# Second layer's quads reordered, its second block pair split in place, and the first layer's last outputs moved among them

## The chip, the cores and the metric

One core of one Trainium2 chip. The time is device microseconds (us) of one execution of the whole program; a kernel's time is the median of its runs.

## The reference

Retention (attention scores times a causal decay table, no softmax), then two feed-forward layers over 2304 tokens, model width 512, inner width 2048:

```python
scores = scale * np.matmul(q, k.transpose(0, 1, 3, 2))
ret = scores * Dmat[None, :, :, :]
x = np.matmul(ret, v)                      # to [2304, 512]
h = x @ w_in                               # layer 1
g = P(h) / (Q(h) + 1e-06)                  # cubic over 1 + |b0 h| + |b1| h^2
x = g @ w_out
h = x @ moe2_w_in                          # layer 2
g = s * (np.maximum(h, 0.0) ** 2) + b
return g @ moe2_w_out
```

## The kernel before, in words

Every fp32 operand of TensorE (PE) is held as two rounded parts, high and low, and a product is three matmuls: high by low, low by high, high by high (`three`, L377). To split a tile, ScalarE (ACT) copies it to the rounded type and VectorE (DVE) or GpSimd (POOL) subtracts (`lo_on`, L521). Weights come from DRAM as 64-bit words (`raw`); `w_round` (L132) turns them into fp32 in one ACT and three DVE instructions, `w_split` (L147) makes the two parts (ACT copy, POOL subtraction). A raw buffer is loaded again (`next_load`, on the SP queue) when its last reader, a POOL instruction, is done.

**Layer 1** runs 80 units (a token block of 512 or 256 by a slice of 128 inner columns). Unit u computes `h` (`emit_in`, 12 matmuls), then `rational` (L418, ACT, POOL, DVE) makes the parts of g, ending in `gl` on POOL (L436), and `out1` (L454) adds 12 matmuls to the outputs. The outputs of the last units have nothing else beside them: the program lists them first and the second layer behind.

**Layer 2** takes the weights in 16 quads (two slices of 128 by two token blocks of 512), `quad` (L702). Quads 0 to 7 are the first pass, tokens 0 to 1023; quads 8 to 15 the second, tokens 1024 to 2047. The last 256 tokens ride in the first pass (`tail_in`). Quads 0 and 8 are computed plainly (`hs`, 4 blocks of 12 matmuls); the others by seven products of 6 matmuls (`product`, Strassen-Winograd) over sums of blocks of x ("1" to "4") and of weights (S1 to S4). Product 1 goes to bank hA, is copied to hB by ACT, and product 2 adds to hA, so product 2 must wait for that copy. 5 and 6 use hG and hB; 3, 7, 4 add to them. Between products `fill(n)` puts n output groups (`out2`, 6 matmuls each) of the quad before; there are 10 per quad in the first pass and 8 in the second. TensorE's order here is pinned as written. ACT, DVE, POOL and the queues run in the order that a scheduler chose at build time, each strictly in order; `behind(...)` keeps an instruction behind another in that order.

In a first-pass quad the next quad's weights are rounded and split (`cut_first` after product 1, `cut_second` after product 6), the weight sums are built on POOL (`s_sums`, L589) and split (`s_split`, L600), and all are written to DRAM for the second pass (`w_keep`, `s_spill`). Quads 1 to 6 also prepare the second pass's x: `x_keep` (L554) splits a block through temporaries, half a block at a time, and spills it by four POOL-queue DMAs; `x_fetch` reads it back in quads 7 and 8. Sums of x blocks are accumulating DMAs of the POOL queue (`x_sum`, L536).

Of the kernel before, what the change touches and what calls it, by code (L numbers as in the profile page):

```python
# [42 lines left out]
def retention_ffn_kernel(ctx, tc, a, b, s2, b2, w, qkv, maskv, gdec, out):  # L43
# [3 lines left out]
    P = 128  # L47
# [99 lines left out]
    def w_split(kf, pinned=False):  # L147
        rest = tc.keep_in_program_order if pinned else free
        f = w_words(kf)[1].bitcast(F32)
        w_views(kf)  # L150
        i, j = w_place(kf)
        if kf < NF:
            t, n = w_halves[i]
            todo = [(f.rearrange("p (w x) -> p w x", w=2), t[:, :, n:n + 2, :])]
        else:
            todo = [(f[:, DM * x:DM * (x + 1)], w_half(y)) for x, y in enumerate((i, j))]
        for src, dst in todo:
            rest(nc.scalar.copy(dst[:, 0], src))  # L158
            nc.gpsimd.tensor_tensor(out=dst[:, 1], in0=src, in1=f32(dst[:, 0]), op=ALU.subtract)  # L159
# [163 lines left out]
    def ffn(fctx):  # L323
# [117 lines left out]

        def evac1(t0, m, f, e, ps):
# [99 lines left out]
        def x_split(pair, key):  # L542
            for c in range(2):
                h, l = (x[:, c, :] for x in both(key))
# [5 lines left out]
        KEYS = ("11", "12", "1", "22", "21", "3")  # L550
        NEXT = {"12": ("1",), "22": ("3", "2"), "21": ("4",)}
        x_spill = {}

        def x_keep(i, c):  # L554
            key = KEYS[i]
            if c == 0:
                x_spill[key] = spill.tile([P, 2, 2, 512], F32, name=f"xs{key}")
            at = x_at(1, key)[:, c, :]
# [5 lines left out]
            if c == 1:  # L564
                if key in ("11", "22"):
                    x_negate(1, key)
                for x in NEXT.get(key, ()):
                    x_sum(1, x)

        fetched = []  # L570

        def x_fetch(key):
            for x, y in enumerate(both(key, 1)):
                fetched[:] = [nc.gpsimd.dma_start(out=y, in_=x_spill[key][:, x])]
# [14 lines left out]
        def s_sums(q):  # L589
            w1, w2 = (w_words(NF + 2 * q + i)[1].bitcast(F32)[:, 0:DM] for i in range(2))  # L590
            a = {"11": w1[:, 0:256], "12": w1[:, 256:512], "21": w2[:, 0:256], "22": w2[:, 256:512]}
            t = [tmp_tile(2 * q + i, "tt") for i in range(2)]
            s1, s2, s3, s4 = t[0][:, 0:256], t[0][:, 256:512], t[1][:, 0:256], t[1][:, 256:512]
            nc.gpsimd.tensor_tensor(out=s1, in0=a["21"], in1=a["22"], op=ALU.add)
            nc.gpsimd.tensor_tensor(out=s3, in0=a["21"], in1=a["11"], op=ALU.subtract)
            nc.gpsimd.tensor_tensor(out=s2, in0=a["11"], in1=s1, op=ALU.subtract)
            nc.gpsimd.tensor_tensor(out=s4, in0=a["12"], in1=s2, op=ALU.add)
            return t
# [46 lines left out]
        def relu2(u, h, n, on_act):  # L645

            ta = tmp.pop(u, None)
            tt = h
            if ta is None:
                ta = tmp_tile(u, "ta", n)  # L650
            if h is ta or n < 512:
                tt = ta
            nc.scalar.activation(ta, h, AF.Relu)  # L653
            nc.scalar.activation(ta, ta, AF.Square)
            if on_act:
                nc.scalar.activation(tt, ta, AF.Identity, bias=b2_sb, scale=s2_sb)
            else:
                nc.vector.tensor_scalar(tt, ta, s2_sb, b2_sb, op0=ALU.mult, op1=ALU.add)
            gh, gl = g_tiles(u, n)
            return nc.scalar.copy(gh, tt), lo_on(nc.vector, gl, tt, gh)  # L660
# [41 lines left out]
        def quad(q, fills):  # L702
# [17 lines left out]
            if NQ // 2 - 1 <= q < NQ - 1:  # L720
                w_fetch(k + 2)
                w_fetch(k + 3)
            if NQ // 2 <= q < NQ - 1:
                with behind(*fetched):
                    s_fetch(q + 1)

            def prep(c):

                if q <= len(KEYS):
                    x_keep(q - 1, c)  # L730
# [9 lines left out]
            def cut_second():  # L740
# [3 lines left out]
                if rounds:  # L744
                    next(rounds[1], None)
                    w_split(k + 3)
                    t = s_sums(q + 1)
                    for x in (k + 2, k + 3):
                        del w_raw[x]
                        next_load()  # L750
                    with behind(*loads):
                        w_keep(k + 2)
                        w_keep(k + 3)
                    s_split(q + 1, t, 0)
                    return lambda: s_split(q + 1, t, 1)
                return lambda: None

            if q % (NQ // 2) == 0:
                while late:
                    late.pop(0)()  # L760
                fill(4)

                for (i, j), tag, key in zip(((0, 0), (0, 1), (1, 1), (1, 0)), ("hA", "hG", "hB", "hT"), ("1", "3", "2", None)):
# [6 lines left out]
                    done = relu2(("q", q, i, j), ps, 512, True)  # L770
                    with behind(*ends):
                        if key and first:
                            x_split(0, key)
                        if (i, j) == (0, 0):
                            cut_first()
                        if (i, j) == (0, 1):
                            cut_second()()
                    ends[:] = done
                    fill(4 if first else 2)
                    if first and (i, j) == (1, 1):  # L780
                        tail_in(q, 0, "o")
                with behind(*ends):
                    x_split(pas, "4")
                if not first:
                    x_fetch("1")
                    x_fetch("3")
# [5 lines left out]
            hB = ps_h.tile([P, 512], F32, tag=("hT", "hB")[q % 2], name=f"hB{q}")  # L792
# [3 lines left out]
            def renew(*keys):  # L796
                if last:
                    for x in keys:
                        x_fetch(x)
# [6 lines left out]
            product(q, 5, hG, True)  # L806
            g5 = tmp_tile(q, "tq")
            ends[:] = [nc.scalar.copy(g5, hG)]
            while late:
                late.pop(0)()  # L810
            fill(2)
            product(q, 6, hB, False)
            ends.append(nc.vector.tensor_tensor(out=hG, in0=hB, in1=g5, op=ALU.add))
            with behind(*ends):
                if last:
                    x_split(1, "2")
                cut_rest = cut_second()
            fill(2)
            product(q, 2, hA, False)
            ends[:] = relu2(("q", q, 0, 0), hA, 512, True)  # L820
            renew("21")
            with behind(*ends):
                prep(0)
            fill(1 + first)
            product(q, 3, hG, False)
            relu2(("q", q, 0, 1), hG, 512, True)
            renew("22")
            fill(1 + first)
# [3 lines left out]
            sum22 = nc.vector.tensor_tensor(out=tmp[u], in0=hB, in1=g5, op=ALU.add)  # L832
            relu2(u, tmp[u], 512, first)
            cut_rest()
            with behind(*ends):
                prep(1)
            fill(2)
# [4 lines left out]
            renew("12")  # L842
            ends[:] = [sum22, sum22]
# [4 lines left out]
        def outs_of(q):  # L848
            return [lambda j=j, e=e: out2(q, j, e) for j in (1, 0) for e in range(4)] + \
# [6 lines left out]
        for u in range(NU):  # L856
# [6 lines left out]
            for x in outs_at[u]:  # L863
                for e in range(NC):
                    out1(x, e)
            if final[0:1024].all() and sums:
# [12 lines left out]
        assert first_rounds and not sums  # L879
        rest = [lambda x=x, e=e: out1(x, e, pe) for x in outs_at[NU] for e in range(NC)]  # L880
# [93 lines left out]
```

## Time and profile before

| what | value |
|---|---|
| time, median of 3 runs | 878.95 us (877.92 to 880.23) |
| the profiled execution's own time | 880.4 us, span 878.6 us |
| granted TensorE clock, mean | 0.995 |
| busy: PE, DVE, ACT, POOL | 848.9, 612.2, 608.6, 439.5 us |

The span runs from the first instruction to the last. PE counts as busy while a matmul is in flight. A row of the trace gives start and duration in us, engine, line, operation, what it writes and reads, and in brackets how long the engine sat idle before it and what it waited for.

### The profile page before, as it was taken

The page shows a single profiled execution, that of the slowest core. Times are in us where ns is not written, and L with a number is a line of the kernel's source. Part 1 is how long each engine was busy: PE and PEld are TensorE (multiplying, and loading weights), DVE is VectorE, ACT ScalarE, POOL GpSimd, SP SyncE. Part 2 cuts the span into 40 slices and gives each one's busy share as a digit, 9 for nine tenths or more (in the row PEclk, how much of TensorE's full clock was granted, in tenths as well). Part 3 has the DMA queues.
Part 4 walks back from the last instruction along what each step waited for, and adds up shares of the span by engine and source line. Part 5 has one row for each costly group of instructions (what it writes and reads, how often), then busy time and mean ns, then how long its engine had stood idle before and what let it go on. Part 6 is the DMA issues. An engine that isn't in the chain of part 4 may idle for free.

```text
span 878.6 us, 12889 instructions
## 1 busy us (share of the span) xinstructions
PE 848.9 (97%) x4812; PEld 715.1 (81%) x4812; DVE 612.2 (70%) x892; ACT 608.6 (69%) x1027; POOL 439.5 (50%) x381
## 2 busy tenths in 40 slices
PE   6989999999999999999998999999989999999998
PEld 5988788788888888888886787878778888888886
DVE  3886886997888887968958856777777423444445
ACT  1333998986878876778878788786767657444553
POOL 2795564575665664656767734555357511111100
PEclk9999999999999999999999999999999999999999
DMA  9992110111111100101113268655889994444402
GB/s 342 371 351 117 49 49 1 48 48 49 49 41 57 49 19 30 48 1 49 48 48 60 42 234 305 216 185 201 290 286 370 401 348 150 144 144 144 144 1 96
DMA packets 44207, 123.59 MB, mean 141 GB/s; under 512 B 4464, under 2 KB 4976, under 8 KB 39152
## 3 DMA queue, kind: packets, MB, share of 16 engines
q1 hardware_dynamic: 28096, 81.86, 25.8%
q0 software_dynamic: 16048, 40.90, 15.3%
q8 instruction: 38, 0.62, 0.3%
q14 instruction: 25, 0.20, 0.1%
HBM read 83.42 MB, written 35.13 MB: 135 GB/s over the span
## 4 chain that ended last, share of the span: by engine, by line
PE 70%; DVE 10%; DMA 6%; ACT 6%; POOL 4%; issue 3%; SPq 0%; POOLq 0%; ACTq 0%; DVEq 0%
PE o L380 19%; PE h L380 18%; PE p L380 15%; PE hB L380 4%; DMA raw<-in_w_dram 3%; PE hG L380 3%; PE hA L380 3%; DVE wm L141 2%; PE sc L239 2%; PE pv L270 2%; DVE raw L144 2%; POOL w L159 2%; PE pv L262 1%; PE hs L380 1%; ACT wm L138 1%
## 5 line engine op out<-in xcount | busy, mean ns | idle before, releaser
L380 PE MATMUL h<-xh,w 128*128 128x512 f32 (+1 forms) x640 | 184.7, 370 | 0.0
L380 PE MATMUL o<-gh,w 128*128 128x512 f32 (+1 forms) x592 | 166.4, 367 | 0.0
L424 POOL TENSOR_TENSOR tq<-tq,ta 128x512 f32<-128x512 f32 (+1 forms) x80 | 100.5, 1256 | 99.6 <-ACT tq L423 99.3
L380 PEld LDWEIGHTS h<-xh,w 128*128 128x128 f32 x640 | 117.4, 190 | 20.6
L380 PE MATMUL p<-w,gh 128*128 128x512 f32 x336 | 122.8, 391 | 0.0
L683 DVE TENSOR_TENSOR acc<-acc,p 128x512 f32<-128x512 f32 x126 | 85.2, 683 | 53.6 <-PE p L380 52.1
L380 PE MATMUL h<-xl,w 128*128 128x512 f32 (+1 forms) x320 | 119.2, 372 | 3.3 <-DVE tt L433 3.2
L380 PEld LDWEIGHTS o<-gh,w 128*128 128x128 f32 x592 | 106.9, 189 | 18.0
L159 POOL TENSOR_TENSOR w<-raw,w 128x512 fp32r<-128x512 f32 (+1 forms) x48 | 84.4, 1764 | 55.7 <-ACT w L158 47.9
L436 POOL TENSOR_TENSOR gl<-tt,gh 128x512 fp32r<-128x512 f32 (+1 forms) x74 | 93.3, 1262 | 35.4 <-ACT gh L435 24.8
L380 PE MATMUL o<-gl,w 128*128 128x512 f32 (+1 forms) x296 | 108.3, 367 | 1.5 <-POOL gl L436 1.5
L380 PE MATMUL p<-w,gx 128*128 128x512 f32 x360 | 99.0, 391 | 0.2 <-ACT ta L653 0.2
L380 PEld LDWEIGHTS p<-w,gx 128*128 128x128 f32 x360 | 67.9, 189 | 14.8 <-ACT ta L653 0.7
L431 DVE SCALAR_TENSOR_TENSOR tt<-tt,aneg,h 128x512 f32<-128x512 f32 (+1 forms) x80 | 55.1, 689 | 35.5 <-ACT h L430 34.9
L380 PEld LDWEIGHTS p<-w,gh 128*128 128x128 f32 x336 | 63.4, 189 | 13.2
L380 PEld LDWEIGHTS h<-xl,w 128*128 128x128 f32 x320 | 60.6, 189 | 15.3 <-DVE tt L433 2.9
L426 DVE TENSOR_TENSOR tt<-tt,h 128x512 f32<-128x512 f32 (+1 forms) x80 | 50.2, 628 | 27.6 <-ACT tt L425 27.4
L428 ACT ACTIVATE ta<-tq,lnb 128x512 f32<-128x512 f32 (+1 forms) x80 | 54.6, 682 | 18.3 <-POOL tq L424 18.0
L380 PE MATMUL p<-w,gl 128*128 128x512 f32 x168 | 65.8, 391 | 1.0 <-DVE gl L522 1.0
L380 PEld LDWEIGHTS o<-gl,w 128*128 128x128 f32 x296 | 55.8, 189 | 11.0 <-POOL gl L436 1.9
L423 ACT ACTIVATE tq<-ta,babs 128x512 f32<-128x512 f32 (+1 forms) x80 | 61.9, 774 | 3.8 <-DVE h L432 3.8
L619 POOL DMA_DIRECT2D w<-ws x32 | 22.8, 712 | 82.9 <-PE hA L380 30.5
(137 smaller groups left out, 1815.6 us busy)
## 6 DMA issues: line engine op xcount, KB each, us to landing
raw<-in_w_dram SPq DMA_DIRECT2D x32, 1024.0 KB, 5.6
ws<-w SPq DMA_DIRECT2D x32, 512.0 KB, 11.1
w<-ws POOLq DMA_DIRECT2D x32, 512.0 KB, 5.7
xT<-in_qkv_dram SPq DMA_DIRECT2D x16, 576.0 KB, 8.4
sf<-ss POOLq DMA_DIRECT2D x7, 1024.0 KB, 5.2
xs<-tt POOLq DMA_DIRECT2D x24, 256.0 KB, 6.7
vn<-in_qkv_dram SPq DMA_DIRECT2D x16, 320.0 KB, 8.5
out_dram<-acc SPq DMA_DIRECT2D x18, 256.0 KB, 3.5
```

The source lines that it names most:

```text
L141: rest(nc.vector.scalar_tensor_tensor(out=t, in0=t, scalar=3, in1=lo, op0=ALU.logical_shift_left, op1=ALU.bitwise_or))
L144: rest(nc.vector.scalar_tensor_tensor(out=hi, in0=hi, scalar=0x80000000, in1=t, op0=ALU.bitwise_and, op1=ALU.bitwise_or))
L159: nc.gpsimd.tensor_tensor(out=dst[:, 1], in0=src, in1=f32(dst[:, 0]), op=ALU.subtract)
L380: yield nc.tensor.matmul(ps, lhsT=lh, rhs=rh, start=start and x == 0, stop=stop and x == 2, skip_group_check=True)
L423: nc.scalar.activation(tq, ta, AF.Identity, bias=babs[:, 0:1], scale=babs[:, 1:2])
L424: nc.gpsimd.tensor_tensor(out=tq, in0=tq, in1=ta, op=ALU.mult)
L426: nc.vector.tensor_tensor(out=tt, in0=tt, in1=h, op=ALU.mult)
L428: nc.scalar.activation(ta, tq, AF.Ln, bias=lnb, scale=QS)
L431: nc.vector.scalar_tensor_tensor(out=tt, in0=tt, scalar=aneg[:, 0:1], in1=r, op0=ALU.add, op1=ALU.mult)
L436: nc.gpsimd.tensor_tensor(out=gl, in0=tt, in1=f32(gh), op=ALU.subtract)]
L619: nc.gpsimd.dma_start(out=w_half(i), in_=w_spill[kf - NF, x])
L683: nc.vector.tensor_tensor(out=at, in0=at, in1=ps, op=ALU.add)
```

## The change

Five parts. (1) In the Strassen quads product 2 comes right after product 1 and two fills; the order is 1, 2, 5, 6, 3, 7, 4, with fills 2, 2, 2, 2, 1 in the first pass and 2, 1, 1, 2, 2 in the second. (2) `cut_first` moves behind product 6 and `cut_second` behind product 7; within it the first half of the weight sums is split before the second weight tile. (3) `x_keep`, `x_fetch` and their spill are gone: quad 7 splits "11", "21", "22", "12" of the second pair straight into the slots that its own products have left, issues the block sums there, and quad 8 splits "1", "3", "2", "4"; quad 8's blocks run in another order, with its outputs between. (4) The outputs of the last three units of layer 1 become fills of quad 0 (`hs00` runs ahead of most of them); some of the last splits go from POOL to DVE (`tail_lo`), and the third and fourth block sums are issued later. (5) A layer-1 weight tile is subtracted on POOL in two halves.

```diff
         if kf < NF:
             t, n = w_halves[i]
-            todo = [(f.rearrange("p (w x) -> p w x", w=2), t[:, :, n:n + 2, :])]
+            nc.scalar.copy(t[:, 0, n:n + 2, :], f.rearrange("p (w x) -> p w x", w=2))
+            for x in range(2):
+                dst = t[:, :, n + x, :]
+                nc.gpsimd.tensor_tensor(out=dst[:, 1], in0=f[:, DM * x:DM * (x + 1)], in1=f32(dst[:, 0]), op=ALU.subtract)
+            return
...
-                nc.gpsimd.tensor_tensor(out=xl[:, e, r], in0=at, in1=f32(xh[:, e, r]), op=ALU.subtract)
+                tail_lo[:] = [lo_on(nc.vector if m < 512 or e % 2 else nc.gpsimd, xl[:, e, r], at, xh[:, e, r])]
...
-        def x_keep(i, c):
-            key = KEYS[i]
...
-            h, l = (tmp_tile(4 * i + 2 * c + x, "tt").bitcast(F32R) for x in range(2))
-            nc.scalar.copy(h, at)
-            lo_on(nc.gpsimd, l, at, h)
-            for x, y in enumerate((h, l)):
-                nc.gpsimd.dma_start(out=x_spill[key][:, x, c], in_=f32(y))
...
+                    t = s_sums(q + 1)
+                    s_split(q + 1, t, 0)
                     w_split(k + 3)
-                    t = s_sums(q + 1)
                     for x in (k + 2, k + 3):
                         del w_raw[x]
                         next_load()
...
+                tags = ("hA", "hB", "hG", "hT") if first else ("hA", "hT", "hG", "hB")
+                order = ((0, 0), (0, 1), (1, 1), (1, 0)) if first else ((0, 0), (1, 0), (0, 1), (1, 1))
...
+                    if not first:
+                        split = relu2(("q", q, i, j), ps, 512, True, wait=True)
+                        fill((4, 4, 2, 0)[n])
+                        done = split()
...
             product(q, 1, hA, True)
-            ends[0] = nc.scalar.copy(hB, hA)
-            with behind(*ends):
-                cut_first()
-            renew("11")
+            nc.scalar.copy(hB, hA)
+            while late:
+                late.pop(0)()
+            n1, n2, n3, n4, n5 = (2, 2, 2, 2, 1) if first else (2, 1, 1, 2, 2)
+            fill(n1)
+            product(q, 2, hA, False)
+            split = relu2(("q", q, 0, 0), hA, 512, True, wait=True)
+            fill(n2)
+            ends[:] = split()
+            if last:
+                with behind(*ends):
+                    x_split(1, "11")
+                    x_negate(1, "11")
+                x_sum(1, "1")
+                with behind(*ends):
+                    x_split(1, "21")
             product(q, 5, hG, True)
...
+            fill(n3)
             product(q, 6, hB, False)
...
+            with behind(*ends):
+                cut_first()
+            fill(n4)
             product(q, 3, hG, False)
...
             product(q, 7, hB, False)
...
+            with behind(*ends):
+                cut_second()
             relu2(u, tmp[u], 512, first)
...
+            fill(n5)
             if first:
                 tail_in(q, 0, "o")
             product(q, 4, hB, False)
...
-            if final[0:1024].all() and sums:
+            if final[0:1024].all() and len(sums) > (1 if u == NU - 1 else 2):
...
-        rest = [lambda x=x, e=e: out1(x, e, pe) for x in outs_at[NU] for e in range(NC)]
+        rest = [lambda x=x, e=e: out1(x, e, pe) for x in range(NU - 3, NU) for e in range(NC)]
```

Three places in the order. **TensorE, end of layer 1** (o74 and o77 are output banks of units 74 to 78, hs00 and hs01 blocks of quad 0, gl78/gh78 and gx parts of g). Before:

```order
L380 MATMUL o77_2_4763<-gx_4106,w4_1052 128x512 x3
L380 MATMUL o77_3_4764<-gx_4106,w4_1052 128x512 x3
L380 MATMUL o77_0_4761<-gl78_4710,w0_80 128x512
L380 MATMUL o77_0_4761<-gh78_4709,w0_80 128x512 x2
L380 MATMUL o77_1_4762<-gl78_4710,w0_80 128x512
```

Now:

```order
L383 MATMUL hs00_4792<-xh_78,w0_80 128x512 x2
L383 MATMUL o74_0_4638<-gx_4122,w0_80 128x512 x3
L383 MATMUL o74_1_4639<-gx_4122,w0_80 128x512 x3
L383 MATMUL o74_2_4640<-gx_4122,w0_80 128x512 x3
L383 MATMUL o74_3_4641<-gx_4122,w0_80 128x512 x3
L383 MATMUL o77_0_4822<-gx_4122,w4_1055 128x512 x3
L383 MATMUL o77_1_4823<-gx_4122,w4_1055 128x512 x3
L383 MATMUL o77_2_4824<-gx_4122,w4_1055 128x512 x3
L383 MATMUL o77_3_4825<-gx_4122,w4_1055 128x512 x3
L383 MATMUL hs01_4838<-xl_79,w0_80 128x512
```

A block of quad 0 now stands before the outputs of unit 76, another between those of units 77 and 78.

**ACT, turn from quad 2 to quad 3** (ta, tt temporaries, ht the tail's bank, raw23 and w0 the weight tile of quad 3). Before:

```order
L653 ACTIVATE ta115_5545<-hB2_5262 128x512
L660 CAST gh114_5495<-ta114_5491 128x256
L654 ACTIVATE ta115_5545<-ta115_5545 128x512
L653 ACTIVATE ta117_5553<-ht5_5505 128x256
L656 ACTIVATE hB2_5262<-ta115_5545,b2_sb_75,s2_sb_74 128x512
L802 COPY hB3_5519<-hA3_5518 128x512
```

Now:

```order
L640 CAST gx_4122<-ta116_5407 128x512
L634 ACTIVATE ta114_5471<-ta114_5471,b2_sb_75,s2_sb_74 128x256
L161 CAST w0_80<-raw23_5184 128x512 x2
L640 CAST gh114_5475<-ta114_5471 128x256
L631 ACTIVATE ta115_5516<-hB2_5264 128x512
L785 COPY hB3_5507<-hA3_5506 128x512
```

The copy of hA to hB comes one instruction after the read of the last quad's hB, not five, and the casts of the second weight tile now stand ahead of it.

**SP queue, a first-pass quad** (ss3 the spilled weight sums of quad 3, ws40 to ws43 spilled weight parts, raw24 and raw25 loads for quad 4). Before:

```order
L608 DMA ss3_5352<-xh_78 128x512
L126 DMA raw25_5340<-in_w_dram 128x1024
L608 DMA ss3_5352<-xl_79 128x512
L126 DMA raw24_5085<-in_w_dram 128x1024
L614 DMA ws40_5087<-w0_80 256x1x512
```

Now:

```order
L586 DMA ss3_5420<-xh_78 128x512
L126 DMA raw25_5429<-in_w_dram 128x1024
L126 DMA raw24_5186<-in_w_dram 128x1024
L592 DMA ws40_5188<-w0_80 256x1x512
L592 DMA ws41_5190<-w4_1055 256x1x512
```

The two loads now follow each other directly.

## Rows read from the trace of the kernel before

**Rows 1.** The page: busy us of each engine over the span (share), instructions.

```profile
PE 848.9 (97%) x4812; PEld 715.1 (81%) x4812; DVE 612.2 (70%) x892; ACT 608.6 (69%) x1027; POOL 439.5 (50%) x381
```

**Rows 2.** Busy time by stretch: start:end, length, engines, PE clock, DMA share, GB/s.

```profile
82.03:470.66 388.63, 385.29 (x1861) 324.75 (x1861) 315.26 (x483) 322.18 (x532) 240.48 (x181) 1.00 0.11 39
470.66:500.85 30.19, 26.73 (x134) 22.18 (x133) 25.52 (x37) 21.63 (x41) 20.88 (x20) 1.00 0.37 70
500.85:696.37 195.52, 187.61 (x885) 154.93 (x884) 135.57 (x173) 149.83 (x267) 103.14 (x112) 0.99 0.79 267
696.37:863.67 167.30, 167.30 (x740) 138.56 (x739) 75.22 (x115) 90.37 (x148) 21.79 (x32) 1.00 0.49 157
863.67:878.60 14.93, 11.04 (x49) 8.82 (x47) 6.24 (x10) 2.60 (x4) 0.00 (x0) 0.94 0.38 142
```

**Rows 3.** Waits of PE: who for whom, us in total, times, longest.

```profile
PE hB L380 <- DVE ta L832: 2.8, 3, 1.1
PE hG L380 <- DVE xl L522: 2.7, 2, 2.5
...
PE o L380 <- POOL gx L436: 2.0, 1, 2.0
...
PE o L380 <- POOL gl L436: 1.5, 1, 1.5
```

**Rows 4.** PE in order of time: first matmul of quads 6, 7 and 8.

```profile
639.92 0.40 PE L380 MATMUL hA<-xl,w 128*128 128x512 f32 x1
...
670.33 0.40 PE L380 MATMUL hA<-xl,w 128*128 128x512 f32 x1
...
696.37 0.63 PE L380 MATMUL p<-w,gx 128*128 128x512 f32 x2
```

**Rows 5.** ACT: a raw tile's landing starts the rounding, two quads in turn.

```profile
569.04 1.16 ACT L138 ACTIVATE wm<-raw 128x1024 f32<-128x1024 f32 x1 [2.85 <-DMA raw<-in_w_dram]
...
596.60 1.17 ACT L138 ACTIVATE wm<-raw 128x1024 f32<-128x1024 f32 x1 [3.00 <-DMA raw<-in_w_dram]
```

**Rows 6.** POOL, quad 3: from the weight sums' start to their last; one spilled split between.

```profile
580.07 0.86 POOL L594 TENSOR_TENSOR tt<-raw 128x256 f32<-128x256 f32 x1 [3.50 <-DVE raw L144]
...
584.96 1.74 POOL L522 TENSOR_TENSOR tt<-acc,tt 128x512 fp32r<-128x512 f32 x1
586.64 0.56 POOL L563 DMA_DIRECT2D xs<-tt  x1
587.22 0.75 POOL L597 TENSOR_TENSOR tt<-raw,tt 128x256 f32<-128x256 f32 x1
```

**Rows 7.** SP queue, the same place: issues of the two raw loads.

```profile
585.02 0.33 SPq L126 DMA_DIRECT2D raw<-in_w_dram  x1
...
588.00 0.33 SPq L126 DMA_DIRECT2D raw<-in_w_dram  x1
```

**Rows 8.** DVE: one operation alone, and beside a busy POOL.

```profile
570.24 1.22 DVE L141 SCALAR_TENSOR_TENSOR wm<-wm,raw 128x1024 uint32<-128x1024 uint32 x1
...
575.52 2.14 DVE L141 SCALAR_TENSOR_TENSOR wm<-wm,raw 128x1024 uint32<-128x1024 uint32 x1 [1.13 <-ACT wm L138]
...
639.93 2.88 DVE L522 TENSOR_TENSOR gx<-ta,gx 128x512 fp32r<-128x512 f32 x1 [1.80 <-ACT gx L660]
```

**Rows 9.** PE and ACT, quad 3: end of product 1, and the copy that product 2 needs.

```profile
558.72 0.39 PE L380 MATMUL hG<-xl,xh 128*128 128x512 f32 x1
...
562.36 0.55 ACT L802 COPY hB<-hA 128x512 f32<-128x512 f32 x1
```

**Rows 10.** ACT groups, 500 to 697 us: count, busy, mean ns.

```profile
L158 ACT CAST w<-raw 128x512 fp32r<-128x512 f32 x26 | 16.0, 664 | 12.7 <-DVE raw L144 12.7
...
L681 ACT COPY acc<-p 128x512 f32<-128x512 f32 x10 | 6.0, 616 | 0.0
```

**Rows 11.** POOL groups, layer 1: a weight tile's subtraction, whole and half.

```profile
L159 POOL TENSOR_TENSOR w<-raw,w 128x1024 fp32r<-128x1024 f32 x13 | 32.9, 2532 | 6.6 <-ACT w L158 6.5
...
L159 POOL TENSOR_TENSOR w<-raw,w 128x512 fp32r<-128x512 f32 x4 | 5.3, 1317 | 1.2 <-ACT w L158 1.2
```

More of the change, by code (lines that the diff above doesn't have):

```diff
@@ L543, in x_split @@
             for c in range(2):
-                h, l = (x[:, c, :] for x in both(key))
+                h, l = (x[:, c, :] for x in both(key, pair))
                 at = x_at(pair, key)[:, c, :]
@@ L658, in relu2, with split @@
                 nc.vector.tensor_scalar(tt, ta, s2_sb, b2_sb, op0=ALU.mult, op1=ALU.add)
-            gh, gl = g_tiles(u, n)
-            return nc.scalar.copy(gh, tt), lo_on(nc.vector, gl, tt, gh)
+            def split():
+                gh, gl = g_tiles(u, n)
+                return nc.scalar.copy(gh, tt), lo_on(nc.vector, gl, tt, gh)
+            return split if wait else split()
         out_units = {}
@@ L723, in quad @@
             if NQ // 2 <= q < NQ - 1:
[L724 to L730, printed above, removed]
+                s_fetch(q + 1)
             def cut_first():
@@ L803, in quad @@
+            product(q, 5, hG, True)
+            g5 = tmp_tile(q, "tq")
+            ends[0] = nc.scalar.copy(g5, hG)
+            fill(n3)
+            product(q, 6, hB, False)
+            ends[1] = nc.vector.tensor_tensor(out=hG, in0=hB, in1=g5, op=ALU.add)
             with behind(*ends):
                 cut_first()
-            renew("11")
[L806 to L824, printed above, removed]
@@ L825, in quad @@
-            product(q, 3, hG, False)
-            relu2(("q", q, 0, 1), hG, 512, True)
-            renew("22")
-            fill(1 + first)
+            fill(n4)
+            product(q, 3, hG, False)
+            ends[:] = relu2(("q", q, 0, 1), hG, 512, True)
+            if last:
+                with behind(*ends):
+                    x_split(1, "22")
+                    x_negate(1, "22")
             product(q, 7, hB, False)
@@ L832, in quad @@
             sum22 = nc.vector.tensor_tensor(out=tmp[u], in0=hB, in1=g5, op=ALU.add)
+            ends[1] = sum22
+            with behind(*ends):
+                cut_second()
             relu2(u, tmp[u], 512, first)
[L834 to L837, printed above, removed]
+            if last:
+                with behind(*ends):
+                    x_split(1, "12")
+                x_sum(1, "3")
+                x_sum(1, "2")
+                w_fetch(k + 2)
+                w_fetch(k + 3)
+            fill(n5)
             if first:
@@ L848, in outs_of @@
         def outs_of(q):
-            return [lambda j=j, e=e: out2(q, j, e) for j in (1, 0) for e in range(4)] + \
+            return [lambda j=j, e=e: out2(q, j, e) for j in ((0, 1) if q == NQ // 2 else (1, 0)) for e in range(4)] + \
                    ([lambda e=e: out2(q, 2, e) for e in range(2)] if q < NQ // 2 else [])
@@ L863, in ffn @@
             for x in outs_at[u]:
-                for e in range(NC):
-                    out1(x, e)
-            if final[0:1024].all() and sums:
+                if x < NU - 3:
+                    for e in range(NC):
+                        out1(x, e)
+            if final[0:1024].all() and len(sums) > (1 if u == NU - 1 else 2):
                 x = sums.pop(0)
@@ L878, in ffn @@
                     pass
-        assert first_rounds and not sums
-        rest = [lambda x=x, e=e: out1(x, e, pe) for x in outs_at[NU] for e in range(NC)]
+        assert first_rounds and sums == ["4"]
+        rest = [lambda x=x, e=e: out1(x, e, pe) for x in range(NU - 3, NU) for e in range(NC)]
         w_split(NF + 1)
```

74 lines of the change are left out of this document (29 added, 45 removed).

## The prediction

> **What bounds the kernel now.** I read the page first: TensorE is busy 848.9 of 878.6 us [rows 1], so at most 29.7 us are open to any reordering, and the question is where they lie. The busy time by stretch answers it [rows 2]. The second pass is full: 167.30 of 167.30 us, 123 groups of six matmuls at 1.36 us. Layer 1 from 82 us on is idle for 388.63 - 385.29 = 3.3 us in all. Two stretches are left. At the end of layer 1 (470.66 to 500.85) TensorE is idle for 30.19 - 26.73 = 3.5 us, and the list of waits names the whole of it: 2.0 and 1.5 us for the low halves of g that POOL makes [rows 3], in a place where nothing else is queued. The other is quads 1 to 7, 195.52 us. What they would take without waits is read from quad 7, which prepares no further weights: 696.37 - 670.33 = 26.04 us [rows 4]. Seven of these are 182.3 us, so 13.2 us are lost there: 7.9 as idle time and the rest at a lower clock and in slowed matmuls (the stretch's granted clock is 0.99, and quad 6, which holds the longest wait, 2.5 us for a split of the weight sums, takes 670.33 - 639.92 = 30.4 us [rows 2 to 4]). The sum that can be won is 3.5 + 13.2 = 16.7 us.
>
> What holds the quads is seen from ACT: each waits for a raw weight tile from DRAM before it rounds, 2.85 and 3.00 us, and these landings are 596.60 - 569.04 = 27.56 us apart [rows 5]. That is a closed loop, and it is longer than 26.04: landing, two roundings, POOL's sums (580.07 to 587.97 [rows 6]), then the load, issued at 588.00 and landed at 596.60, 8.6 us [rows 5, 7]. TensorE runs at the pace of this loop.
>
> **The change part by part.** The sum is made against the profiled execution, 880.4 us (span 878.6 and 1.8 around it), which lies 1.45 us above the median of 878.95; I carry differences over to the median.
>
> *End of layer 1: -3.5.* Blocks of quad 0, two groups or 2.7 us each, now stand between the late outputs. Unit 76's, 77's and 78's outputs come 2.7, 2.7 and 5.4 us later than before, against waits of 2.0 and 1.5 us [rows 3]; POOL also has two accumulating DMAs behind, not ahead of, the last two subtractions. Both waits go.
>
> *First copy of quad 1: +1.4.* What is late next is ACT. Between the end of quad 0's third block and product 2 of quad 1 TensorE has 1.4 + 2.7 + 2.9 + 1.4 + 2.7 = 11.1 us of work. In that time ACT has some 20 instructions ahead of the copy hA to hB: two blocks of four at about 0.65, the tail block, eight tail and split casts, one rounding of 1.16 [rows 5], about 12 us, and then the copy, 0.55 [rows 9]. So 1.4 late; between 0 and 3.
>
> *Quad 1: +1.5.* ACT takes 149.83 / 7 = 21.4 us per quad [rows 2]; the two casts of the spilled split that go are 1.3 (by the 664 ns of a like cast [rows 10]), and quad 1's own first copies of the outputs are ten of 0.616 [rows 10], 5.3 more than their share in that mean. That is 25.4 of 26.04 us, for an engine that runs strictly in order. Between 0 and 3; the middle.
>
> *Quads 1 to 7: -13.2, and the raw loop +2.0.* The POOL part of the loop loses a subtraction of 1.74 and a DMA issue of 0.56 [rows 6]: 27.56 - 2.3 = 25.3. Two things lengthen it. The two loads are now issued 0.4 us apart instead of 2.98 [rows 7], so the one that is needed first no longer has the other's head start ahead of it: between 0 and 2.6 more. And both stand on SP behind the spill of the first sums, which waits for an ACT cast: 0 to 1. So 25.3 to 28.9; I take 26.8, a little under the middle, since the spilled splits' writes go from the same moment. Against 26.04 that is 0.76 per quad and 3.8 over five loads. Since the roundings now stand 12 us later in the quad, the loop starts with a reserve: by the durations above the copy for product 2 is done 28.3 to 30.0 us after a quad's start, and product 2 stands at 30.1. I credit 1.8, which leaves 2.0; between 0 and 7.
>
> The loop's DVE part shows a second price. A rounding step took 1.22 us alone and 2.14 beside a busy POOL, and one subtraction 2.88 us [rows 8]. The Trainium skill (Perfetto Trace Analysis, Optimizing Scalar/DVE Operations) says that GpSimd and VectorE share a read port of the on-chip memory, so moving work between them may not help; the trace agrees in these three numbers. By that rule the last splits that go from POOL to DVE win nothing, and the first copy would be at its upper bound, 3 us and not 1.4. I stay with 1.4, because what sets that copy is ACT's queue.
>
> *Weight sums for quad 7: +0.5.* POOL has three reloads for quad 8 ahead of these sums, and they wait for quad 6's last matmuls. Product 5 now comes after product 2 and four fills, 6.8 us later than before, where it waited 2.5 [rows 3]. Between 0 and 2.5.
>
> *Second pass: 0.* The splits of the second pair are ten on DVE and two on POOL, twelve ACT casts as before, in a stretch where ACT is busy 90.37 and DVE 75.22 of 167.30 us [rows 2]. Spill and fetch, 24 and 12 DMAs, go. The four block sums are a chain on POOL's queue that has all of quad 8, 18 groups or 24.5 us, before it is needed. If the cover went, the price is a wait at quad 9's product 5; 0 to 3.
>
> *Layer 1: 0.* Two halves of 1.317 for one 2.532 [rows 11]: 0.1 more POOL per tile, POOL busy 240 of 389 us. The last stretch, after 863.67, is the same.
>
> **Sum:** -16.7 + 1.4 + 1.5 + 2.0 + 0.5 = -11.3. 878.95 - 11.3 = **867.6 us**.
>
> **The rivals.**
> *All waits go.* The raw loop fits into 26 us and ACT is never late: -16.7, 862.3 us. For it: the reckoned loop's lower bound is 25.3. Against it: ACT's full quad 1.
>
> *The raw loop still binds.* Both loads share the queues and the loop is 28.5: 2.5 per quad over five loads, less the reserve, is 10.7 instead of 2.0, and 876.3 us; at 27.7 it is 872. For it: 8.6 us per load already now. Against it: less traffic. The Trainium skill (DMA: Bandwidth & Descriptors, Issuing engines are not separate DMA queues) says that transfers run on the same 16 engines and interleave, whichever engine issued them; by it two loads issued together finish together, which is this rival. No row here shows two of them issued together.
>
> *Slower: product 2 waits for the copy in every quad.* Before, products 5 and 6 and four fills, 8.2 us, lay between product 1 and product 2; now two fills, 2.7. In quad 3 of before, product 1 ended at 558.72 and the copy at 562.36 + 0.55 = 562.91, 4.2 us later [rows 9]; left there, with two fills between, it would make product 2 wait 1.5 us. In the changed order four instructions have moved behind the copy, but the casts of the second weight tile stand ahead of it and wait for the rounding, which is later. Each of the seven quads then pays what the copy is late, and the weights after it too. From 2.4 us per quad (16.7 / 7) all that was won is gone; at 2.8, with the other terms, it is 882 us. Against it: the reckoned reserve of 0.1 to 1.8 us.
>
> *It does not do what it says:* the scheduler holds the roundings where they were, or the waits at the end of layer 1 move on to unit 79. The order shows neither. About 877.
>
> **How the numbers follow.** The forecast has 0.50, all waits gone 0.17, the raw loop still binding 0.18, the late copy 0.09, no effect 0.06. A measurement of this kernel tells about 0.3% (2.6 us) from no change. Faster by more than that: the first three but for the end of the third, 0.84. Within it: 0.08. Slower: 0.08. The range for 8 in 10 takes in the case without waits, with a little below it for a gain in layer 1's one stall, and most of the binding loop: 861 to 875 us.
>
> **What would show it.** Right: no wait for g's low halves at the end of layer 1; quads 2 to 6 at 26.0 to 26.8 us and quad 1 at about 27.5; the first copy of quad 1 as a wait of 1 to 2 us; the second pass still full at 167 us. The raw loop binding shows as ACT waiting for the raw tiles ahead of the first rounding and quads of 27 us and more. The late copy shows as PE waiting for ACT ahead of product 2 in each quad. The prediction is wrong if TensorE stands idle in the second pass, or if layer 1 before 470 us takes another time by more than 2 us.

## The result, and the profile after

The changed kernel takes 867.52 us (median of 4 runs, 867.36 to 867.68) against 879.43 for the kernel before, run on the same chip: the ratio is 0.9867, with a 95% interval of 0.9849 to 0.9884, or 11.9 us. The forecast was 867.6. The sum came out, but not each of its terms, and the experiments show that the parts of the change are not independent either.

The page of the kernel after, span and busy time:

```profile
span 865.6 us, 12863 instructions
PE 843.7 (97%) x4812; PEld 712.7 (82%) x4812; DVE 618.0 (71%) x910; ACT 602.3 (70%) x1027; POOL 406.1 (47%) x343
```

PE was busy for 848.9 us before [rows 1]; the same 4812 matmuls now take 843.7; the granted clock is 1.00 in every stretch from layer 1 to the end of the second pass. Busy time of the kernel after by stretch, cut at the same places of the program as [rows 2] (columns as there):

```profile
81.50:470.13 388.63, 384.77 (x1863) 323.32 (x1861) 314.45 (x485) 321.43 (x531) 238.33 (x190) 1.00 0.12 39
470.13:497.60 27.47, 26.38 (x135) 22.25 (x134) 25.65 (x41) 22.99 (x44) 15.10 (x13) 1.00 0.36 68
497.60:683.36 185.76, 183.50 (x884) 153.89 (x883) 137.16 (x178) 138.97 (x256) 71.46 (x64) 1.00 0.65 227
683.36:850.64 167.28, 167.28 (x739) 138.56 (x738) 79.47 (x121) 94.30 (x158) 26.64 (x36) 1.00 0.48 142
850.64:865.60 14.96, 11.04 (x49) 8.82 (x47) 6.71 (x10) 2.60 (x4) 0.00 (x0) 0.97 0.38 141
```

The end of layer 1 with quad 0 lost 2.7 us (30.19 to 27.47), quads 1 to 7 lost 9.8 (195.52 to 185.76), the second pass is full as before, and the start-up was 0.5 shorter in this execution (the end of layer 1 lies between 469.5 and 472.0 us in the 14 profiles of this study, so half a microsecond there means nothing). These make the 13.0 us between the two spans.

PE in order of time, kernel after: first matmul of quads 1, 2, 3, 7 and 8.

```profile
497.60 0.40 PE L383 MATMUL hA<-xl,w 128*128 128x512 f32 x1
...
525.50 0.39 PE L383 MATMUL hA<-xl,w 128*128 128x512 f32 x1
...
551.54 0.39 PE L383 MATMUL hA<-xl,w 128*128 128x512 f32 x1
...
655.70 0.39 PE L383 MATMUL hA<-xl,w 128*128 128x512 f32 x1
...
683.36 0.39 PE L383 MATMUL hs<-xl,w 128*128 128x512 f32 x1
```

Quad 1 takes 27.90 us. Quads 2 to 6 take 26.04 each, (655.70 - 525.50) / 5, exactly the length without waits that the prediction read from quad 7 before [rows 4]. Quad 7 takes 27.66. What is left of waits between 470 and 690 us, after (who for whom, us in total, times, longest):

```profile
PE hG L383 <- DVE xl L527: 1.3, 2, 0.9
PE ht L383 <- DVE xl L527: 1.1, 1, 1.1
PE hG L383 <- ACT xh L583: 0.7, 1, 0.7
PE hA L383 <- ACT hB L785: 0.3, 1, 0.3
```

Those for g's low halves on POOL [rows 3] are gone. New is `ht`, quad 0's first tail block, behind the last low halves of x that DVE now makes. Both rows of hG are splits of weight sums: the low half (DVE) in quads 1 and 7, the high half (ACT) in quad 7. These waits cost more than their length: 1.2 us in quad 1 make it 1.86 us longer than 26.04, and 1.05 us in quad 7 make it 1.62 longer, at a granted clock of 1.00.

The loop of the raw tiles after, from three views. ACT, two roundings of a quad and the first of the next:

```profile
591.45 1.16 ACT L138 ACTIVATE wm<-raw 128x1024 f32<-128x1024 f32 x1 [3.56 <-DMA raw<-in_w_dram]
...
599.44 1.15 ACT L138 ACTIVATE wm<-raw 128x1024 f32<-128x1024 f32 x1
...
617.28 1.13 ACT L138 ACTIVATE wm<-raw 128x1024 f32<-128x1024 f32 x1 [3.35 <-DMA raw<-in_w_dram]
```

SP's queue, and POOL's last weight sum, after:

```profile
608.72 1.49 SPq L126 DMA_DIRECT2D raw<-in_w_dram  x2
```

```profile
608.65 1.20 POOL L575 TENSOR_TENSOR tt<-raw,tt 128x256 f32<-128x256 f32 x1
```

Of the two loads the second, issued when the last sum ends (609.85), is the one that the next quad rounds first; the tile view gives 5.5 and 7.4 us to landing for the pair, and 609.9 + 7.4 is 617.3, where ACT starts. Before, that load was issued at 588.00 and took 8.6 [rows 5, 7]. ACT still waits 3.4 us, but 14 us into the quad, with nothing urgent behind it. The sums and the next load need the second tile's rounding too (599.44), which waits for no DMA: it stands in ACT's queue behind what follows product 3. So TensorE paces the loop, not the loop TensorE.

### The profile page after: what moved, and what is told of

Read it like the earlier page. It is cut to its first block, busy times and chain, and to the rows that moved or that the text cites. A ratio compares the mean times of both kernels' runs of the same rounds, so it can differ in the third digit from the quotient of the medians.

```text
span 865.6 us, 12863 instructions
## 1 busy us (share of the span) xinstructions
PE 843.7 (97%) x4812; PEld 712.7 (82%) x4812; DVE 618.0 (71%) x910; ACT 602.3 (70%) x1027; POOL 406.1 (47%) x343
## 4 chain that ended last, share of the span: by engine, by line
PE 84%; DVE 6%; ACT 4%; POOL 2%; DMA 2%; issue 2%; SPq 0%; POOLq 0%; ACTq 0%
PE p L383 21%; PE o L383 21%; PE h L383 18%; PE hB L383 6%; PE hG L383 4%; PE hA L383 4%; PE ht L383 2%; PE hs L383 2%; PE sc L242 2%; PE pv L273 2%; DMA vn<-in_qkv_dram 1%; DVE xl L527 1%; PE pv L253 1%; PE pv L265 1%; POOL w L157 1%
## 5 line engine op out<-in xcount | busy, mean ns | idle before, releaser
L162 POOL TENSOR_TENSOR w<-raw,w 128x512 fp32r<-128x512 f32 x32 | 46.3, 1461 | 79.4 <-ACT w L161 79.4
L425 ACT ACTIVATE ta<-h 128x512 f32<-128x512 f32 (+1 forms) x80 | 44.2, 552 | 22.4 <-PE h L383 21.4
```

The source lines that it names most:

```text
L425: nc.scalar.activation(ta, h, AF.Abs)
```

## The experiments

In each, "quads" is the time from quad 1's first matmul to quad 8's: 195.52 us before, 185.76 after.

**One part alone: the end of layer 1** (e1_bound: the kernel before, with this part).

```diff
-            for x in outs_at[u]:
+                if x < NU - 3:
...
-        rest = [lambda x=x, e=e: out1(x, e, pe) for x in outs_at[NU] for e in range(NC)]
+        rest = [lambda x=x, e=e: out1(x, e, pe) for x in range(NU - 3, NU) for e in range(NC)]
```

> The kernel before, with only the end of layer 1 and quad 0 of the change (outputs of the last three units as fills of quad 0, the last splits partly on DVE). Theory: this part is worth its own stall, the stretch from layer 1's last group to quad 1 falls from 30.2 to about 27.5 us, the quads stay as before at 27.5 us and more, and the time is 2.7 us under the kernel before. Rival: the raw loop of the quads runs at its own pace and takes the gain back, quad 1 waits for its weights instead; then the time is within 1 us of the kernel before.

Measured: 884.5 us against 880.4, ratio 1.0051 (1.0036 to 1.0066), so slower. The stretch did fall, to 27.46 us; but quad 1 takes 35.96 (497.40 to 533.36). The row of quad 1, PE in order of time and by stretch:

```profile
503.90 0.79 PE L380 MATMUL hG<-xl,xh 128*128 128x512 f32 x1 [4.95 <-ACT xh L606]
507.43 0.79 PE L380 MATMUL hG<-xh,xl 128*128 128x512 f32 x1 [2.73 <-DVE xl L523]
```

```profile
497.40:533.36 35.96, 28.28 (x128) 23.05 (x127) 22.16 (x23) 26.24 (x49) 18.77 (x18) 0.91 0.56 179
```

Both theories fell, the rival only in its size and its object: not the raw loop but quad 1's weight sums. They are now made beside quad 0's third block instead of its second, and product 5, which needs them, stands right behind product 1 in the old order. 7.7 us of waits cost 9.9. The granted clock of that quad is 0.91 on the mean; from 503.5 to 510.3 us it is 0.50, the lower of the two levels (1.2 and 2.4 GHz), and the matmul after each wait takes 0.79 us there, where it takes 0.50 at the upper level.

**The order of the products alone undone** (e4_p2late: after, product 2 behind product 6).

```diff
-            product(q, 2, hA, False)
             product(q, 5, hG, True)
...
             product(q, 6, hB, False)
...
+            product(q, 2, hA, False)
```

> The changed kernel, with product 2 back behind product 6. Theory: product 2's place costs and brings nothing by itself in quads 2 to 6 (26.04 us either way); in quad 1 and quad 7 at most 1 us; the time is within 1.5 us of the changed kernel. Rival (product 2 ahead is what lets the sums come later without a wait): product 5 again waits for the split of the weight sums, 0.5 to 2 us in each quad, and the time is 3 to 10 us over the changed kernel.

The fills keep their new places, here and wherever this order is undone below, so product 5 stands two output groups, 2.7 us, behind product 1, where before it followed directly.

Measured: 886.4 us, ratio 1.0071 (1.0056 to 1.0086); quads 204.94. The rival held, and by more than it said: with the sums late and product 5 early, all seven quads wait for the split of the weight sums. PE's waits in quads 1 to 7, 13.6 us:

```profile
PE hG L383 <- ACT xh L583: 8.5, 6, 3.2
PE hG L383 <- DVE xl L527: 5.1, 7, 2.1
```

**The place of the rounding alone undone** (e3_early: after, `cut_first` behind product 1's copy, `cut_second` behind product 6; within it the first half of the weight sums is again split behind the second weight tile).

```diff
-            nc.scalar.copy(hB, hA)
+            ends[0] = nc.scalar.copy(hB, hA)
+            with behind(*ends):
+                cut_first()
...
             with behind(*ends):
-                cut_first()
+                cut_rest = cut_second()
```

> The changed kernel, with the weight rounding back at its earlier places: the first tile's behind the copy after product 1, the second's and the sums behind product 6. Theory (the spilled split was what made the loop too long): the loop is shorter than 26.04 us wherever it stands, quads 2 to 6 stay at 26.0 to 26.4 us, and the time is within 2 us of the changed kernel, 866 to 870. Rival (the place of the rounding is what counts: ACT, in strict order, waits for a raw tile while TensorE needs its copies): quads 2 to 6 take 27 us and more, 872 us and more.

Measured: 866.83 us (866.60 to 867.27), ratio 0.9849 (0.9832 to 0.9865); quads 184.77. The theory held: the later place brings nothing. Quads 4 to 7 take 26.0 to 26.1 us, quad 7's wait is gone (its sums come earlier), and quads 2 and 3 pay 0.4 and 0.1. The intervals of this kernel and of the change overlap, so whether it is the faster one by some 0.7 us stays open.

**Both orders undone, without the spill** (e9_early_p2late: the edits of the two above).

> The changed kernel with both order changes of its quads undone: product 2 back behind product 6, and the rounding back at its earlier places; the spilled split stays out, and the new end of layer 1 stays. In e4_p2late the loop was landing to second rounding 9.3 us, to the next load 9.3 us, load 8.8 us, 27.5 in all, since product 2 lay between the two roundings. Theory (it is the pair of late rounding and late product 2 that costs, and without the spill the old order would fit): quads 2 to 6 take 26.0 to 26.5 us, only quad 1 pays for its late weight sums (5 to 8 us), and the time is 871 to 876 us. Rival (product 2 has to be ahead whatever the rounding does): quads of 27 us and more, 880 us and more.

Measured: 874.76 us, ratio 0.9949 (0.9933 to 0.9964); quads 191.86. The theory held: quads 4 to 7 run at 26.04 in the old order, and quad 1 takes 34.61, for the same two waits as in e1_bound, at other lengths:

```profile
506.04 0.49 PE L383 MATMUL hG<-xl,xh 128*128 128x512 f32 x1 [3.19 <-ACT xh L583]
508.64 0.79 PE L383 MATMUL hG<-xh,xl 128*128 128x512 f32 x1 [2.11 <-DVE xl L527]
```

So with early rounding product 2 ahead is worth 7.1 us (191.86 to 184.77), nearly all of it in quad 1, where it covers the sums that the new end of layer 1 makes late.

**The spill taken out, the orders and the end of layer 1 as before** (e13_spill_only: before, with the second pair split at its pass; small things of the change stay in: the new places of the fills, the new quad 8, part (5), and the order of two weight sums, which the change also swaps).

```diff
-            renew("11")
...
-                prep(0)
...
+            if last:
+                with behind(*ends):
+                    x_split(1, "11")
+                    x_negate(1, "11")
```

> The kernel before, with one part of the change alone: the second pair is split at its pass, the spill and its reloads are gone; the end of layer 1, the order of the products and the places of the rounding are those of before. e9_early_p2late showed quads at 26.04 us without the spill in the old order. Theory (the spill was all that held the quads): quads 2 to 7 at 26.0 to 26.5 us, the two waits of 2.0 and 1.5 us at the end of layer 1 stay, quad 1 at 27 to 28.5 us, and the time is 866.5 to 870 us, so that the other parts of the change bring 0 to 3 us together. Rival (old end of layer 1 and old order still cost more than their waits): 871 us and more.

Measured: 874.72 us, ratio 0.9940 (0.9928 to 0.9953). In the quads the theory held in the main: 187.32 us, 8.2 of the change's 9.8, with quads 5 to 7 at 26.04, but quads 2 to 4 at 27.57, 26.77 and 26.66. The time is that of the rival, since the stretch at the end of layer 1 took 33.8 us instead of 30.2. PE in order of time there:

```profile
475.12 3.01 PE L383 MATMUL o<-gx,w 128*128 128x512 f32 x12 [0.75 <-POOL gx L439]
481.74 5.49 PE L383 MATMUL o<-gx,w 128*128 128x512 f32 x12 [3.60 <-POOL gx L439]
```

The longest wait for g's low half was 2.0 before [rows 3] and is 3.6 here, and the twelve matmuls behind it take 5.49 us instead of 3.01, at a granted clock of 0.50 from 480.7 to 487.5 us. Of the 3.6 us that the stretch is longer than before, 0.9 are waits; the other 2.7 are matmuls that take longer, at that clock. What these instructions compute is the same as before, but the scheduler has placed layer 1's last instructions on ACT and POOL in another order. Why it chose so is open; the parts that stay in are not ruled out.

**The spill put back** (e2_keep: after, with the split's work and writes in quads 1 to 6; e10_early_keep: the same on e3_early).

```diff
+            at = x_at(1, key)[:, c, :]
+            h, l = (tmp_tile(4 * i + 2 * c + x, "tt").bitcast(F32R) for x in range(2))
+            nc.scalar.copy(h, at)
+            lo_on(nc.gpsimd, l, at, h)
+            for x, y in enumerate((h, l)):
+                nc.gpsimd.dma_start(out=x_spill[key][:, x, c], in_=f32(y))
```

> The changed kernel, with the spilled split of the second pair put back into quads 1 to 6 as extra work that nobody reads: per quad two casts on ACT, two subtractions on POOL and four DMAs issued by POOL. Theory (the raw loop was too long because of this work): the loop is again longer than 26.04 us, quads 2 to 6 take 27.0 to 27.6 us with ACT waiting for raw tiles, and the time is 5 to 8 us over the changed kernel, 872 to 875. Rival (the order of the products and the later rounding made the reserve): quads 2 to 6 stay at 26.0 to 26.3 us and the time is within 1.5 us of the changed kernel.

> Product 2 ahead and early rounding (as e3_early), with the spilled split of the second pair put back into quads 1 to 6 as extra work that nobody reads. Theory (the spilled split lengthens the loop wherever the rounding stands, by its DMAs beside the loads): quads of 27 to 29 us, loads that take over 10 us from issue to landing, 876 to 884 us. Rival (early rounding leaves enough reserve for it): within 2 us of e3_early, 866 to 869.

Measured: 884.13 us (1.0044, 1.0029 to 1.0059), quads 200.77; and 880.92 (1.0017, 1.0005 to 1.0030), quads 199.37. Both theories held in that the spill makes the quads longer wherever the rounding stands, but the size in the first was far too small: the spill costs 15.0 and 14.6 us in the quads. (The 12.9 and 8.7 us in the expectations are counted from the pair's first issue to ACT's start. The load that is needed is the second; by its own issue it is 10.1 and 7.5.) In e2_keep, rounding on ACT, two quads in turn; then POOL between the sums; then SP's load; then the tile view of that pair of loads:

```profile
602.69 1.18 ACT L138 ACTIVATE wm<-raw 128x1024 f32<-128x1024 f32 x1 [7.48 <-DMA raw<-in_w_dram]
...
631.86 1.20 ACT L138 ACTIVATE wm<-raw 128x1024 f32<-128x1024 f32 x1 [7.12 <-DMA raw<-in_w_dram]
```

```profile
589.44 1.79 POOL L527 TENSOR_TENSOR tt<-acc,tt 128x512 fp32r<-128x512 f32 x1
591.17 0.56 POOL L566 DMA_DIRECT2D xs<-tt  x1
591.75 0.77 POOL L589 TENSOR_TENSOR tt<-raw,tt 128x256 f32<-128x256 f32 x1
```

```profile
592.55 0.33 SPq L126 DMA_DIRECT2D raw<-in_w_dram  x1
```

```profile
DMA to landing us min/median/max: 6.7/8.4/10.1
```

The loop is 631.86 - 602.69 = 29.2 us. The last sum stands behind 2.3 us of the split's work on POOL, and the load issued after it lands 10.1 us later instead of 7.4. ACT, waiting 7 us for it, starts the rounding so late that VectorE's sum after product 7 is late too: PE waits for that in four quads, 7.8 us in all, and the granted clock of three of them is 0.94 or 0.95.

**The two halves of the spill** (e12_keep_nodma: casts and subtractions without the DMAs; e16_dma_only: DMAs from the accumulator, without casts and subtractions).

```diff
+            nc.scalar.copy(h, at)
+            lo_on(nc.gpsimd, l, at, h)
...
+                    nc.gpsimd.dma_start(out=x_spill[key][:, x, c], in_=x_at(1, key)[:, c, :])
```

> As e2_keep, with the casts and subtractions of the spilled split, but without its four DMAs per quad. In e2_keep a load took 12.9 us from issue to landing instead of 8.7. Theory (the writes beside the loads are what lengthens the loop): loads at 8.7 us again, quads 2 to 6 at 26.0 to 26.7 us, the time within 3 us of the changed kernel, 867 to 870. Rival (the 1.8 us on POOL and the casts on ACT are what counts): loads at 8.7, and still quads of 27 us and more, 873 us and more.

> The changed kernel, with four DMAs of 256 KB per quad that write the accumulator to DRAM, issued by POOL behind each quad's weight sums in quads 1 to 6; no cast and no subtraction. Theory (it is the writes beside the loads that made the loop too long): loads take 11 to 13 us from issue to landing instead of 8.7, quads 2 to 6 take 27.5 us and more, 874 to 884 us. Rival (the writes alone do no harm): loads at 8.7 to 9.5 us, within 2 us of the changed kernel.

Measured: 875.77 us (0.9957, 0.9943 to 0.9971) and 869.81 us (0.9880, 0.9867 to 0.9894). Quads 2 to 6 take 26.0 to 26.7 us in the first and 26.0 to 26.4 in the second. The needed load lands after 7.3 us there, and after 8.4 here:

```profile
DMA to landing us min/median/max: 6.3/6.8/7.3
```

```profile
DMA to landing us min/median/max: 5.9/7.2/8.4
```

So neither half alone makes quads 2 to 6 longer by more than 0.7 us, and the expectation for e16_dma_only, that the writes do it, fell. With one half the tiles are rounded 26.15 us (567.22 to 593.37) and 26.00 us apart (568.48 to 594.48), at TensorE's pace; with both, 29.2. The second run is not an exact half: all its writes are issued behind the last sum, where e2_keep issues two of the four ahead of the needed load, one of them between the sums. What the writes cost in that place isn't shown.

What e12_keep_nodma loses is in another place, quad 7, at 36.00 us. PE and DVE in order of time, and the stretch:

```profile
671.15 0.80 PE L383 MATMUL hG<-xl,xh 128*128 128x512 f32 x1 [4.23 <-ACT xh L593]
```

```profile
660.08 4.70 DVE L527 TENSOR_TENSOR gl<-ta,gh 128x256 fp32r<-128x256 f32 x1 [1.08 <-ACT gh L650]
...
668.33 0.41 DVE L527 TENSOR_TENSOR gl<-ta,gh 128x256 fp32r<-128x256 f32 x1
```

```profile
656.23:692.23 36.00, 30.08 (x127) 23.66 (x126) 22.97 (x30) 23.09 (x44) 13.26 (x16) 0.91 0.73 241
```

POOL has the sums, a reload for quad 8, the weight tile and the split there one behind another, from 657.94 to 665.37 us. Beside them one VectorE subtraction takes 4.70 us that takes 0.41 some 8 us later. ACT stands 3.79 us waiting for it, with the cast of the weight sums behind it in its queue, and PE waits for that cast. That is the place at which the prediction had put 0.5 us, for the reloads alone.

**VectorE's share of the last splits undone** (e11_early_tail, on e3_early).

```diff
-                tail_lo[:] = [lo_on(nc.vector if m < 512 or e % 2 else nc.gpsimd, xl[:, e, r], at, xh[:, e, r])]
+                tail_lo[:] = [lo_on(nc.gpsimd, xl[:, e, r], at, xh[:, e, r])]
```

> As e3_early, with the last low halves of the tail block all subtracted by POOL, as before the change, and none by VectorE. Theory: the wait of 1.08 us ahead of quad 0's first tail block comes from these subtractions in VectorE's queue and goes, 0.5 to 1 us under e3_early. Rival: POOL has them later still, and the wait grows to 2 us and more.

Measured: 871.17 us, 0.9906 (0.9887 to 0.9925), so some 4 us over e3_early. Neither theory had it: the wait of 1.08 fell to 0.59, but two others came, 2.1 us at the end of layer 1 and 1.1 in quad 2, and the wait for quad 1's copy grew from 0.28 to 1.9. The edit also gives POOL the odd quarters of the first two token blocks, which stand ahead of g's low halves in its queue. PE's waits in that kernel:

```profile
PE o L383 <- POOL gx L439: 2.1, 1, 2.1
PE hA L383 <- ACT hB L786: 1.9, 1, 1.9
PE p L383 <- DVE gl L527: 1.1, 1, 1.1
PE ht L383 <- POOL xl L527: 0.6, 1, 0.6
```

**Two attempts on quad 1** (e14_hold4, e15_hold14, both on e3_early).

```diff
-                with behind(*ends):
+                with behind(*(s_done[0] if first else ends)):
                     x_split(pas, "4")
```

> As e3_early, with the last split of quad 0 (key 4, two casts on ACT and two subtractions on VectorE, needed only by product 4 of quad 1) issued behind the first split of the weight sums on both engines. Theory (these four stand in the queues ahead of the copy for product 2 and of the weight sums, 2.2 us on ACT and 4.6 on VectorE for two such splits): the waits of 0.28 and 0.98 us in quad 1 go and quad 1 takes 26.0 to 26.8 us instead of 27.96, 1 to 2 us under e3_early. Rival (the sums come late from POOL anyway): same as e3_early within 0.5 us.

> As e14_hold4, with the split of key 1 in quad 0 also behind the last low halves of the tail block. Theory (two subtractions of key 1, 3.07 us on VectorE, stand ahead of the tail's): the wait of 1.08 us ahead of the first tail block goes, up to 1 us under e14_hold4. Rival (VectorE is full here and the rounding for quad 1 behind them comes later instead): the wait moves to quad 1's weight sums, no gain or up to 1.5 us worse.

Measured: 868.04 us (0.9870, 0.9855 to 0.9886) and 868.76 (0.9871, 0.9858 to 0.9885); neither beats e3_early. e14_hold4 did what it was meant to in quad 1, 26.07 us, and lost it in quad 2, 29.26, and quad 3, 27.54. In quad 2 PE waits in three places that were full before:

```profile
527.78 0.50 PE L383 MATMUL hA<-xl,w 128*128 128x512 f32 x1 [0.51 <-ACT hB L786]
541.21 0.50 PE L383 MATMUL hG<-xl,xh 128*128 128x512 f32 x1 [0.90 <-DVE hG L809]
547.99 0.50 PE L383 MATMUL hB<-xl,w 128*128 128x512 f32 x1 [0.97 <-DVE ta L822]
```

With TensorE 2 us earlier, ACT's first rounding of quad 2 waits 3.9 us for its raw tile, as against 1.0 in e3_early. In e15_hold14 the tail's wait fell from 1.08 to 0.19 and quad 1 took 0.9 us more than in e3_early. The time is within what its rival said, 0.7 us over e14_hold4, but the waits of quad 1 are not at the weight sums: 0.86 us for the copy and 1.30 for VectorE's sum ahead of product 4. This looks as if the first turns of the loop were bound by when the first loads land, so that a wait removed ahead of them moves; no run varies those loads by themselves.

## Why the prediction was right, and where its terms were not

*End of layer 1, -3.5:* measured -2.7. Both waits went, as said. What the step missed is the next thing late, 1.09 us for the tail's low halves: the last splits were counted in ACT's queue, by their casts, and not in VectorE's, by their subtractions. Also missed: taken alone this part loses (e1_bound).

*First copy of quad 1, +1.4, and quad 1, +1.5:* measured 0.26 and in all 27.90 - 26.04 = 1.86 instead of 2.9. The step took ACT's queue as the bound. The larger wait, 0.94 us, is for the low half of the weight sums on VectorE, whose queue is full there from 499.28 us on, with four subtractions at 1.15 us each beside POOL's sums, where one takes 0.68 alone.

The Trainium skill (Perfetto Trace Analysis, Optimizing Scalar/DVE Operations) warns that GpSimd and VectorE share a read port, so that moving work between them may not help. By that rule the subtractions that went from POOL to VectorE would win nothing. The runs don't bear it out here: with them back on POOL (e11_early_tail) the kernel is some 4 us slower. They do show single instructions of the two engines slowing each other: the VectorE subtraction of 4.70 us in e12_keep_nodma takes 0.41 alone.

*Raw loop, +2.0:* measured 0.0. The size was off because of the load's landing, reckoned up to 2.6 us longer for two loads issued 0.4 us apart; they are 1.2 apart in quads 3 to 5, and the needed one takes 7.4 to 7.5 us there, 1.0 to 1.2 shorter than before. The reserve credited to the later rounding, 1.8, isn't what did it, since e3_early has none of it and does as well. What did it is named in the prediction too, the spilled split, but it was priced by POOL's 2.3 us, and its writes only by a choice a little under the middle. Writes behind the sums lengthen the load by 1 us (e16_dma_only), the whole split by 2.4 to 2.6 (e2_keep), and only the whole split breaks the cover: 15 us.

The Trainium skill (DMA: Bandwidth & Descriptors, Issuing engines are not separate DMA queues) has all transfers on the same 16 engines, interleaved; I had taken from it that two loads issued together finish together. The trace doesn't agree with that reading: issued 1.2 us apart (582.77 and 583.93), the two took 5.9 and 7.5 us to landing, so the second landed 2.8 us behind the first.

*Weight sums for quad 7, +0.5:* measured 1.62, at the place named, but by another path. The reloads do stand ahead of the sums on POOL, and the sums start at 656.26. But these are ready (662.11) before ACT casts them (664.09); the chain behind the wait runs over ACT, which had stood 1.12 us for a VectorE subtraction that took 2.04 us beside POOL and takes 0.41 elsewhere:

```profile
609.77 0.41 DVE L527 TENSOR_TENSOR gl<-ta,gh 128x256 fp32r<-128x256 f32 x1
...
656.92 2.04 DVE L527 TENSOR_TENSOR gl<-ta,gh 128x256 fp32r<-128x256 f32 x1 [0.33 <-ACT gh L640]
```

The prediction read such collisions from [rows 8] and gave them no price here. *Second pass, 0* and *layer 1, 0:* as said.

*The rivals:* that the raw loop still binds fell with quads 2 to 6 at 26.04. That product 2 waits for the copy in every quad fell too: after quad 1 there is no such wait. Its sign was the wrong way round: not product 2 ahead is the danger, product 2 behind is (e4_p2late, e9_early_p2late). The prediction priced this reordering only as a risk and never asked what product 5 would do without it. So the sum came out at the right place because the change had all its parts; the two parts measured nearly alone, +4.1 us (e1_bound) and -5.4 (e13_spill_only), give no hint of it. That it hit the median to 0.1 us is luck. By stretch the change won 12.5 us and not 11.3: the raw loop and quad 1 came out 2.0 and 1.0 better than forecast, the end of layer 1 and quad 7 0.8 and 1.1 worse, and the execution that the sum was made against took 1.45 us more than the median from which it was subtracted.

## What to carry to other kernels

A loop of load, work and next load that runs beside the bound engine costs nothing until it is longer than that engine's period, and then it costs its excess in every turn: compare its length with the period, with the other traffic of that moment in it. Parts of a change that feed the same wait are not a sum; before an order is judged, ask which operand would be late without it. A wait on TensorE is dearer than its length, and most where the clock falls with it.

## What the runs showed of the hardware that was not expected

TensorE's waits cost more than their length. In e9_early_p2late 5.3 us of waits made quad 1 8.6 us longer, in e1_bound 7.7 made 9.9, in e12_keep_nodma 5.9 made quad 7 10.0 us longer; in each the granted clock of the quad was 0.90 or 0.91. In the kernel after, waits of 1.1 us and less left it at 1.00 and still cost half as much again. In between both happened: with 1.84 us of waits in e2_keep's quad 4 it was 0.94, with 1.87 in e11_early_tail's quad 1 it was 1.00.

A VectorE subtraction of 128x256 took 0.41 us, and 2.04 (kernel after, quad 7) or 4.70 us (e12_keep_nodma, quad 7) beside a busy POOL.

In quads 3 to 5 a load of 1 MB, the second of its pair, took 7.4 to 7.5 us from issue to landing in the kernel after, 8.4 to 8.6 in e16_dma_only with four more writes of 256 KB behind the last sum, and 9.8 to 10.1 in e2_keep with four such writes around it. The kernel before has four such writes around it too, with the two loads as far apart (2.98 us, against 2.75 in e2_keep), and there it took 8.4 to 8.6. So what made 10 of 8.5 isn't shown.
